# Sliding-window K/V loads as one 128-partition transfer, and four value chunks behind the keys

## The chip, the core and the metric

The kernel runs on one core of one Trainium2 chip; the other cores are idle. The metric is the device time of one launch in microseconds. Five engines matter here: TensorE (PE in the profile), VectorE (DVE), ScalarE (ACT), GpSimd (POOL) and SyncE (SP), which issues nearly all transfers. Sixteen DMA engines carry the transfers between the chip's main memory and the on-chip buffer of 128 partitions.

## The reference

Two attention blocks decode one token for four batches, and their outputs are concatenated. Block A has 32 query heads over 8 key/value heads and looks at the last 2,048 of 8,192 cached positions; block B has 32 key/value heads and looks at all 8,192. The head size is 128.

```
A: W = min(4096, max(256, Sk // 4))                 # 2048
   q = (x @ wq).reshape(B, Sq, Hq, Dh)              # 4, 1, 32, 128
   k = repeat(k_cache[:, :, Sk - W:, :], rep)       # 8 heads, each for 4 query heads
   v = repeat(v_cache[:, :, Sk - W:, :], rep)
   o = softmax(q k^T * Dh ** -0.5) v
   a = o.reshape(B, Sq, Hq * Dh) @ wo               # 4, 1, 512
B: the same with 32 key/value heads, all 8192 positions
return concatenate([a, b], -1)
```

All inputs are bfloat16. The K/V caches that must be read are 33.6 MB for A and 536.9 MB for B; the query and output weights add 8.4 MB each.

## The kernel before

**Chunks.** The work is cut into 72 chunks. Chunks 0 to 7 (A) are one key/value head for all four batches: 64 tiles of 128 positions, 2.10 MB of keys and as much of values. Chunks 8 to 71 (B) are two heads of one batch: 128 tiles, 4.19 MB each of keys and values. A group is eight tiles: 8 groups in an A chunk, 16 in a B chunk.

**Layout.** A partition of a buffer holds 64 consecutive positions of one sequence. In A, batch b lies in partitions 32b to 32b + 31, so a key chunk is loaded by four transfers, one for each batch (L221 to L227). In B two heads take 64 partitions each, and one transfer of 128 partitions loads a chunk (L238).

**For each group** PE transposes eight key tiles into PSUM (`emit_T`, L301), DVE or ACT copies them out (L313 to L317; ACT takes every third), and PE multiplies them with the queries (`emit_S`, L322). A tile's scores are computed against 16 query columns in A (four batches by four heads), and only the columns of a partition's own batch are meant. `scores_out` (L348) therefore copies, for each half chunk, four blocks of 32 partitions with their own four columns.

**Softmax.** `stats_rowmax`, `stats_gmax` and `stats_exp` (L359 to L420) find the maximum over the positions of a row: DVE reduces along the free axis, PE transposes, DVE reduces again, PE spreads the result back. For A, DVE then scales and shifts the scores (L414), ACT takes the exponential in four blocks of 32 partitions (L417), writing each batch's columns into `pba` whose other columns stay zero, and DVE sums over the tiles (L419). The zeros are what keeps the batches apart when PE multiplies values with the probabilities (`emit_pv`, L423), 64 columns at a time of which 16 (A) or 2 (B) are used. `norm_sum`, `norm_out` and `emit_fin` (L443 to L480) divide and multiply with the output weights.

**Order.** The order on PE is written out by group number: transposes of group s, scores of group s - 2, values of an older chunk. Values of a chunk start `PVLAG` groups after the scores end (4 in A, 8 in B). Each engine's queue is in order.

**Buffers.** A ring of ten half-slots of 16 KB a partition (`take`, L184) holds K and V; an A load takes one, a B load two. A load waits until the earlier user of its slot is done: for keys the transposes of their last group, for values the value product. SP issues loads in the order of the list built in L246 to L248: keys of chunk c + 1, then values of chunk c; the values of the last three chunks stand behind all keys. Output weights (`dma_wo`, L209) have three slots: the load for slot use i waits for the product of the chunk that last used it. The first two transfers of query weights use ring slots 8 to 9 and 6 to 7. The last value chunk is loaded in four pieces (64, 32, 16 and 16 tiles, L230 to L237). The values of the third-last chunk may start at group 10 of the last one (L502).

Of the kernel before, what the change touches and what calls it, by code (L numbers as in the profile page):

```python
# [72 lines left out]
def bass_concat_heads__sliding_block_cached__mha_block_cached__decode_kernel(  # L73
        nc, A_x, A_k, A_v, A_wq, A_wo, B_x, B_k, B_v, B_wq, B_wo, out):
    NB = A_x.shape[0]
# [48 lines left out]
    with ExitStack() as es:  # L124
        block = es.enter_context(nc.Block())

        def sb(name, shape, dt):
            return es.enter_context(nc.sbuf_tensor(name, shape, dt))
# [11 lines left out]
        identf = sb("identf", [P, P], F32)  # L140
        onesf = sb("onesf", [P, P], F32)
        onesb = sb("onesb", [P, P], BF16)
        sA = sb("sA", [P, 2, NTA * REP], F32)
        rm = sb("rm", [P, NSM, 4], F32)
        gm = sb("gm", [4, NSM, 4], F32)
        gx = sb("gx", [4, NSM, P], F32)
# [70 lines left out]
        def dma_kv(kind, c):  # L217
            ch = chunks[c]
            T = {("k", 0): A_k, ("k", 1): B_k, ("v", 0): A_v, ("v", 1): B_v}[(kind, ch["ab"])]
            at, waits = take((kind, c), 1 if ch["ab"] == 0 else 2, ("T", ch["s_last"]) if kind == "k" else ("pv", c))  # L220
            if ch["ab"] == 0:  # L221
                PP = P // NB
                for b in range(NB):
                    src = T[b, ch["g"], SkA - W:, :].rearrange("(pp j) d -> pp (j d)", pp=PP)
                    sch.add_dma("sp", lambda e, b=b, src=src: e.dma_start(kv[b * PP:(b + 1) * PP, at, :], src),  # L225
                                "d_h%d" % at, waits=waits, key=(kind, c) if b == NB - 1 else None)
# [18 lines left out]

        loads = [("k", c + 1) for c in range(NC - 1)]  # L246
        for c in range(NC):
            loads.insert(2 * c + 1 if c < NC - 3 else len(loads), ("v", c))  # L248
        wo_next = 0
        for kind, c in loads:  # L250
            dma_kv(kind, c)
# [42 lines left out]
            ms_read[:] = [("q", ab)]  # L294


        def tile_of(kind, c, j):
            at = half_of[(kind, c)]
            return flat(at, chunks[c]["NT"] // NTA)[:, j * P:(j + 1) * P]

        def emit_T(s):  # L301
            c, g = groups[s]
            bank = s % NTRB
            for t in range(TG):
                o = tr[:, bank, t * P:(t + 1) * P]
# [4 lines left out]
                sch.add("pe", lambda e, o=o, i_=i_: e.transpose(o, i_, identb[:, :]),  # L310
                        waits=waits, key=("T", s) if t == TG - 1 else None)
            src, dst = tr[:, bank, :], kt[:, s % NKT, :]
            waits = [("T", s)] + ([("S", s - NKT)] if s >= NKT else [])  # L313
            if s % 3 == 2:
                sch.add("act", lambda e: e.activation(dst, src, ACTF.Copy), waits=waits, key=("ev", s))  # L315
            else:
                sch.add("dve", lambda e: e.tensor_copy(dst, src), waits=waits, key=("ev", s))  # L317

        sc_read = {0: [], 1: []}
        HT = NTA // 2  # L320

        def emit_S(s):  # L322
# [18 lines left out]
                        waits=waits, key=("S", s) if t == TG - 1 else None)  # L341


        def blocks(c):
            U = chunks[c]["U"]
            return [(u, slice(u * (P // U), (u + 1) * (P // U))) for u in range(U)]

        def scores_out(c, half):  # L348

            m = c % 2  # L350
            for u, pp in blocks(c):
                src = sc[pp, half, :].rearrange("p (j x) -> p j x", x=16)[:, :, u * REP:(u + 1) * REP]
                dst = sA[pp, m, half * HT * REP:(half + 1) * HT * REP].rearrange("p (j x) -> p j x", x=REP)
                sch.add("dve", lambda e, src=src, dst=dst: e.tensor_copy(dst, src),  # L354
                        waits=[("S", chunks[c]["s"] + (half + 1) * (HT // TG) - 1)] + ([("exp", c - 2)] if c >= 2 else []),
                        key=("so", c, half) if u == NB - 1 else None)
            sc_read[half] = [("so", c, half)]

        def stats_rowmax(c):  # L359
            ch = chunks[c]  # L360
            m, C = c % NSM, ch["C"]
            if ch["ab"] == 0:
                src = sA[:, c % 2, :].rearrange("p (j c) -> p c j", c=C)
                sch.add("dve", lambda e: e.tensor_reduce(out=rm[:, m, 0:C], in_=src, axis=AX.X, op=ALU.max),
                        waits=[("so", c, 0), ("so", c, 1)], key=("rowmax", c))
                return
            for u, pp in blocks(c):
                src = sc[pp, c % 2, 0:NTB * 2].rearrange("p (j u) -> p u j", u=2)[:, u, :]
                sch.add("dve", lambda e, src=src, pp=pp: e.tensor_reduce(out=rm[pp, m, 0:1], in_=src, axis=AX.X, op=ALU.max),  # L369
                        waits=[("S", ch["s_last"])], key=("rowmax", c) if u == 1 else None)  # L370

        def stats_gmax(c):
            ch = chunks[c]
            m, C, U = c % NSM, ch["C"], ch["U"]
            col = TRM0 + (c % 2) * P
            sch.add("pe", lambda e: e.transpose(ms[0:C, col:col + P], rm[:, m, 0:C], identf[:, :]),  # L376
                    waits=[("rowmax", c), "c_identf"] + ms_read, key=("trm", c))
            src = ms[0:C, col:col + P].rearrange("n (u p) -> n u p", u=U)
# [3 lines left out]
            g = gm[0:C, m, 0:U]  # L382
            gv = bass.AP(g.tensor, g.offset, [g.ap[0], [1, U], [0, P // U]])
            sch.add("dve", lambda e: e.tensor_scalar(out=gx[0:C, m, :].rearrange("n (u p) -> n u p", u=U), in0=gv, scalar1=-scale,  # L384
                                                     scalar2=None, op0=ALU.mult),
                    waits=[("gmax", c)], key=("gx", c))

        def stats_exp(c):
# [10 lines left out]
            pbv = pbt[ab][:, i, 0:ch["NT"] * ch["UC"]].rearrange("p (j x) -> p j x", x=ch["UC"])  # L399
            r = ch["norm"] % NSM  # L400
            if ab == 1:
                for u, pp in blocks(c):
# [9 lines left out]
            nbv = negb[:, m, 0:C]  # L412
            bias = bass.AP(nbv.tensor, nbv.offset, [nbv.ap[0], [0, NTA], [1, C]])
            sch.add("dve", lambda e: e.scalar_tensor_tensor(out=t, in0=t, scalar=scale, in1=bias, op0=ALU.mult, op1=ALU.add),  # L414
                    waits=[("negb", c)], key=("shift", c))
            for u, pp in blocks(c):
                sch.add("act", lambda e, pp=pp, u=u: e.activation(pbv[pp, :, u * C:(u + 1) * C], t[pp], ACTF.Exp),  # L417
                        waits=[("shift", c)] + pw, key=("exp", c) if u == U - 1 else None)
            sch.add("dve", lambda e: e.tensor_reduce(out=rst[0][:, r, :], in_=pbv.rearrange("p j x -> p x j"), axis=AX.X, op=ALU.add),  # L419
                    waits=[("exp", c)] + rs_read[r], key=("rs", c))  # L420


        def emit_pv(c, g):  # L423
# [2 lines left out]
            base = (ch["norm"] % NSM) * 16 + ch["n0"]  # L426
            for t in range(TG):
                j = g * TG + t
                o = po[:, base:base + NW]
                l = tile_of("v", c, j)  # L430
                r = pbt[ch["ab"]][:, c % NPB[ch["ab"]], j * UC:j * UC + NW]
# [60 lines left out]
        for c, ch in enumerate(chunks):  # L492
# [75 lines left out]
```

## Time and profile before

| | |
|---|---|
| median of 3 runs | 1507.73 us (1505.11 to 1511.19) |
| the profiled execution | 1506.58 us |
| its span, first to last instruction | 1504.7 us |
| mean granted TensorE clock | 0.933 |
| PE busy | 1184.0 us (79%) |
| DVE busy | 622.7 us (41%) |
| ACT busy | 443.5 us (29%) |
| POOL busy | 4.5 us (0%) |
| read from main memory | 587.21 MB, 390 GB/s over the span |

The times below come from one execution under the profiler. A page divides the span into 40 slices of 37.6 us; the busy digits are tenths. A row of the table of stages gives, for a stretch from A to B us, the busy time of PE, of its weight loads, of DVE, ACT and POOL with their instruction counts, then the granted clock, the mean busy share of the DMA engines and their rate. A row of the groups gives line, engine, operation, output and input with their shapes, the count, busy time and mean duration, and the idle time of the engine before them with what ended it. A row of the waits gives the waiting engine and line, what released it, the time in total, the number of waits and the longest. A row of the issues gives a transfer, its count, KB each and the median time from issue to landing.

### The profile page before, as it was taken

To read this page: it belongs to the slowest core of one execution; us is meant where nothing else is said; L and a number is where in the kernel's file an instruction comes from. 1 tells how busy PE (TensorE), PEld (TensorE's weight loads), DVE (VectorE), ACT (ScalarE), POOL (GpSimd) and SP (SyncE) were. 2 spreads that over 40 slices of the span, in tenths; PEclk is the share of its full clock that TensorE was granted. 3 is DMA by queue.
4 is the path that set the end of the run, shared out by engine and by line. 5 is a ranking of instruction groups with operands and counts; after the bars stand their busy time and mean duration, and the time that the engine had idled before them with its cause. 6 is when DMAs were issued, how large, how long until landed. Compare 5 with 4: busy or idle time off the path is not lost.

```text
span 1504.7 us, 55575 instructions
## 1 busy us (share of the span) xinstructions
PE 1184.0 (79%) x26704; PEld 1124.8 (75%) x26704; DVE 622.7 (41%) x1211; ACT 443.5 (29%) x651; POOL 4.5 (0%) x12
## 2 busy tenths in 40 slices
PE   3457578878878788887788888788788887888888
PEld 3456468877878788877778877787777877887887
DVE  1344345434444344444444444444444444444443
ACT  0112123322323333332333233233333332332332
POOL 1000000000000000000000000000000000000000
PEclk9677679999999999999999999999999999999999
DMA  9999999999999999999999999999999999999995
GB/s 313 211 215 218 217 339 427 429 429 426 426 428 429 427 424 429 427 427 424 417 421 413 426 426 412 428 412 424 425 418 418 423 425 422 419 419 425 423 424 223
DMA packets 30929, 590.78 MB, mean 393 GB/s; under 512 B 3424, under 2 KB 11632, under 8 KB 11888
## 3 DMA queue, kind: packets, MB, share of 16 engines
q1 hardware_dynamic: 30680, 587.22, 98.2%
q8 instruction: 208, 3.41, 0.9%
q14 instruction: 17, 0.14, 0.0%
q10 hardware_dynamic: 24, 0.01, 0.0%
HBM read 587.21 MB, written 0.01 MB: 390 GB/s over the span
## 4 chain that ended last, share of the span: by engine, by line
DMA 56%; PE 33%; issue 4%; DVE 4%; SPq 2%; another core or an unknown queue 0%; ACT 0%; DVEq 0%
DMA kv<-in_B_k_cache_dram 48%; PE tr L310 15%; PE po L437 8%; PE sc L340 8%; DMA kv<-in_A_k_cache_dram 8%; SPq L225 2%; DVE kt L317 2%; PE ms L392 1%; DVE rm L369 1%; PE ms L376 1%; PE fin L473 0%; DVE rsa L419 0%; ACT pba L417 0%; DVE sA L354 0%
## 5 line engine op out<-in xcount | busy, mean ns | idle before, releaser
L310 PE MATMUL tr<-identb,kv 128*128 128x128 bf16 x8704 | 708.5, 227 | 172.0 <-DMA kv<-in_B_k_cache_dram 83.2
L317 DVE COPY kt<-tr 128x1024 bf16<-128x1024 bf16 x726 | 501.8, 692 | 762.5 <-PE tr L310 759.4
L310 PEld LDWEIGHTS tr<-identb,kv 128*128 128x128 bf16 x8704 | 535.3, 102 | 185.1 <-DMA kv<-in_B_k_cache_dram 89.1
L315 ACT ACTIVATE kt<-tr 128x1024 bf16<-128x1024 bf16 x362 | 370.7, 1024 | 943.8 <-PE tr L310 943.2
L340 PE MATMUL sc<-qs,kt 128*128 128x64 bf16 x8704 | 459.8, 196 | 39.9 <-issue 37.7
L437 PE MATMUL po<-pbb,kv 128*128 128x64 bf16 x8192 | 419.1, 194 | 50.9 <-issue 50.7
L340 PEld LDWEIGHTS sc<-qs,kt 128*128 128x128 bf16 x8704 | 382.8, 101 | 45.2 <-issue 40.1
L437 PEld LDWEIGHTS po<-pbb,kv 128*128 128x128 bf16 x8192 | 319.6, 99 | 63.6 <-issue 63.0
L405 ACT ACTIVATE pbb<-sc,negb 64x128 bf16<-64x128 f32 x128 | 51.5, 402 | 81.8 <-DVE negb L394 80.5
L369 DVE TENSOR_REDUCE rm<-sc 64x1 f32<-64x128 f32 x128 | 36.5, 286 | 17.6 <-PE sc L340 16.7
L376 PE MATMUL ms<-identf,rm 128*1 128x128 f32 (+1 forms) x72 | 20.6, 287 | 20.9 <-DVE rm L369 10.7
L437 PE MATMUL po<-pba,kv 128*128 128x64 bf16 x512 | 32.8, 219 | 1.5 <-issue 1.1
L392 PEld LDWEIGHTS ms<-identf,gx 1*128 1x128 f32 (+1 forms) x144 | 22.2, 192 | 12.4 <-DVE gx L384 6.2
L392 PE MATMUL ms<-identf,gx 1*128 1x1 f32 (+1 forms) x144 | 28.4, 264 | 2.4 <-DVE gx L384 1.8
L437 PEld LDWEIGHTS po<-pba,kv 128*128 128x128 bf16 x512 | 25.7, 115 | 5.2 <-issue 4.7
L473 PE MATMUL fin<-wor,oT 128*4 128x512 bf16 x64 | 18.8, 395 | 13.0 <-DVE oT L453 12.2
L376 PEld LDWEIGHTS ms<-identf,rm 128*1 128x1 f32 (+1 forms) x72 | 6.0, 83 | 30.3 <-DVE rm L369 19.1
L379 DVE TENSOR_REDUCE gm<-ms 1x2 f32<-1x128 f32 (+1 forms) x72 | 19.6, 273 | 13.2 <-PE ms L376 13.2
L405 ACT ACTIVATION_READ_ACCUMULATOR pbb<-sc,negb 64x1 f32 x128 | 23.7, 185 | 0.0
L419 DVE TENSOR_REDUCE rsa<-pba 128x16 f32<-128x1024 bf16 x8 | 15.9, 1993 | 14.0 <-ACT pba L417 14.0
L354 DVE COPY sA<-sc 32x128 f32<-32x128 f32 x64 | 18.2, 285 | 4.9 <-PE sc L340 4.3
L417 ACT ACTIVATE pba<-sA 32x256 bf16<-32x256 f32 x32 | 13.2, 414 | 21.8 <-DVE sA L414 21.3
(31 smaller groups left out, 88.8 us busy)
## 6 DMA issues: line engine op xcount, KB each, us to landing
kv<-in_B_k_cache_dram SPq DMA_DIRECT2D x64, 4096.0 KB, 29.6
kv<-in_B_v_cache_dram SPq DMA_DIRECT2D x63, 4096.0 KB, 32.1
kv<-in_A_k_cache_dram SPq DMA_DIRECT2D x32, 512.0 KB, 38.1
kv<-in_A_v_cache_dram SPq DMA_DIRECT2D x32, 512.0 KB, 41.0
kv<-in_A_wq_dram SPq DMA_DIRECT2D x1, 4096.0 KB, 12.8
kv<-in_B_wq_dram SPq DMA_DIRECT2D x1, 4096.0 KB, 32.9
wor<-in_A_wo_dram SPq DMA_DIRECT2D x8, 512.0 KB, 42.4
wor<-in_B_wo_dram SPq DMA_DIRECT2D x8, 512.0 KB, 32.0
```

What stands on the lines that cost most here:

```text
L225: sch.add_dma("sp", lambda e, b=b, src=src: e.dma_start(kv[b * PP:(b + 1) * PP, at, :], src), "d_h%d" % at, waits=waits, key=(kind, c) if ...
L310: sch.add("pe", lambda e, o=o, i_=i_: e.transpose(o, i_, identb[:, :]), waits=waits, key=("T", s) if t == TG - 1 else None)
L315: sch.add("act", lambda e: e.activation(dst, src, ACTF.Copy), waits=waits, key=("ev", s))
L317: sch.add("dve", lambda e: e.tensor_copy(dst, src), waits=waits, key=("ev", s))
L340: sch.add("pe", lambda e, o=o, l=l, q=q: e.matmul(o, l, q, start=True, stop=True), waits=waits, key=("S", s) if t == TG - 1 else None)
L369: sch.add("dve", lambda e, src=src, pp=pp: e.tensor_reduce(out=rm[pp, m, 0:1], in_=src, axis=AX.X, op=ALU.max), waits=[("S", ch["s_last"]) ...
L376: sch.add("pe", lambda e: e.transpose(ms[0:C, col:col + P], rm[:, m, 0:C], identf[:, :]), waits=[("rowmax", c), "c_identf"] + ms_read, key ...
L379: sch.add("dve", lambda e: e.tensor_reduce(out=gm[0:C, m, 0:U], in_=src, axis=AX.X, op=ALU.max), waits=[("trm", c)], key=("gmax", c))
L392: sch.add("pe", lambda e: e.matmul(ms[:, col:col + C], gx[0:C, m, :], identf[0:C, 0:C], start=True, stop=True), waits=[("gx", c)] + ms_rea ...
L405: sch.add("act", lambda e, src=src, pp=pp, ri=ri, u=u: e.activation(pbv[pp, :, u], src, ACTF.Exp, bias=negb[pp, m, 0:1], scale=scale, accu ...
L437: sch.add("pe", lambda e, o=o, l=l, r=r, j=j: e.matmul(o, l, r, start=(j == 0), stop=(j == ch["NT"] - 1)), waits=waits, key=("pv", c) if j ...
L473: sch.add("pe", lambda e, l=l, r=r, st=st, sp_=sp_: e.matmul(fin[p0:p0 + NB, :], l, r, start=st, stop=sp_), waits=[("oT", c), ("wo", ch["w ...
```

## The change

A sliding chunk is loaded by one transfer of 128 partitions. Partition p now holds batch p mod 4 and the position block p div 4, so the batches are interleaved over the partitions; the rows stay 16 KB. Blocks of 32 partitions can then no longer tell the batches apart, and a mask does it: `mk[p, b]` is 1 where p mod 4 is b. The scores of a half chunk are multiplied with the mask and summed over the four batches (two DVE instructions in place of four copies). ACT takes one exponential of 128 partitions by 256 into a new buffer `eA`; POOL multiplies it with the bfloat16 mask into `pba`, all 16 columns. The sums are taken over `eA` (256 elements a partition) and spread with the mask. The maximum and its spreading follow the new partition order.

Besides, in A every odd group's key copy goes to ACT as well as every third; the lag of A's values goes from 4 to 6 groups; the values of the last four chunks stand behind all keys, start after the last group's transposes, and use 2 columns in place of 64.

```diff
-PVLAG = {0: 4, 1: 8}
+PVLAG = {0: 6, 1: 8}
...
-                PP = P // NB
-                for b in range(NB):
-                    src = T[b, ch["g"], SkA - W:, :].rearrange("(pp j) d -> pp (j d)", pp=PP)
-                    sch.add_dma("sp", lambda e, b=b, src=src: e.dma_start(kv[b * PP:(b + 1) * PP, at, :], src),
-                                "d_h%d" % at, waits=waits, key=(kind, c) if b == NB - 1 else None)
+                src = T[:, ch["g"], SkA - W:, :].rearrange("b (pp j) d -> pp b (j d)", pp=P // NB)
+                sch.add_dma("sp", lambda e: e.dma_start(kv[:, at, :], src), "d_h%d" % at, waits=waits, key=(kind, c))
...
-            loads.insert(2 * c + 1 if c < NC - 3 else len(loads), ("v", c))
+            loads.insert(2 * c + 1 if c < NC - 4 else len(loads), ("v", c))
...
+        idv = identf[:, :].rearrange("p (x b) -> p b x", b=NB)
+        sch.add("dve", lambda e: e.tensor_reduce(out=mk[:, :], in_=idv, axis=AX.X, op=ALU.add), waits=["c_identf"], key="mk")
+        sch.add("dve", lambda e: e.tensor_copy(mkb[:, :], mk[:, :]), waits=["mk"], key="mkb")
...
-            if s % 3 == 2:
+            if s % 3 == 2 or (c < NCA and s % 2 == 1):
...
-            for u, pp in blocks(c):
-                src = sc[pp, half, :].rearrange("p (j x) -> p j x", x=16)[:, :, u * REP:(u + 1) * REP]
-                dst = sA[pp, m, half * HT * REP:(half + 1) * HT * REP].rearrange("p (j x) -> p j x", x=REP)
-                sch.add("dve", lambda e, src=src, dst=dst: e.tensor_copy(dst, src),
...
+            sch.add("dve", lambda e: e.tensor_tensor(
+                out=sel[:, :].rearrange("p (j b c) -> p j b c", b=NB, c=REP),
+                in0=sc[:, half, :].rearrange("p (j b c) -> p j b c", b=NB, c=REP),
+                in1=bcast(mk[:, :], [[0, HT], [1, NB], [0, REP]]), op=ALU.mult),
...
+            sch.add("dve", lambda e: e.tensor_reduce(
+                out=dst, in_=sel[:, :].rearrange("p (j b c) -> p j c b", b=NB, c=REP), axis=AX.X, op=ALU.add),
...
-            for u, pp in blocks(c):
-                sch.add("act", lambda e, pp=pp, u=u: e.activation(pbv[pp, :, u * C:(u + 1) * C], t[pp], ACTF.Exp),
-                        waits=[("shift", c)] + pw, key=("exp", c) if u == U - 1 else None)
-            sch.add("dve", lambda e: e.tensor_reduce(out=rst[0][:, r, :], in_=pbv.rearrange("p j x -> p x j"), axis=AX.X, op=ALU.add),
-                    waits=[("exp", c)] + rs_read[r], key=("rs", c))
+            ev = eA[:, c % 2, :]
+            sch.add("act", lambda e: e.activation(ev, sA[:, c % 2, :], ACTF.Exp),
+                    waits=[("shift", c)] + ([("exp", c - 2), ("rs4", c - 2)] if c >= 2 else []), key=("exp1", c))
+            sch.add("pool", lambda e: e.tensor_tensor(
+                out=pbv.rearrange("p j (b c) -> p j b c", b=NB), in0=bcast(ev, [[C, NTA], [0, NB], [1, C]]),
+                in1=bcast(mkb[:, :], [[0, NTA], [1, NB], [0, C]]), op=ALU.mult),
+                waits=[("exp1", c), "mkb"] + pw, key=("exp", c))
+            sch.add("dve", lambda e: e.tensor_reduce(out=rs4[:, r, :], in_=ev.rearrange("p (j c) -> p c j", c=C), axis=AX.X, op=ALU.add),
+                    waits=[("exp1", c)], key=("rs4", c))
+            sch.add("dve", lambda e: e.tensor_tensor(
+                out=rst[0][:, r, :].rearrange("p (b c) -> p b c", b=NB), in0=bcast(rs4[:, r, :], [[0, NB], [1, C]]),
+                in1=bcast(mk[:, :], [[1, NB], [0, C]]), op=ALU.mult),
+                waits=[("rs4", c)] + rs_read[r], key=("rs", c))
...
-                o = po[:, base:base + NW]
+                n = NW if c < NC - 4 else UC
+                o = po[:, base:base + n]
...
-            if c == NC - 3:
-                v0 = max(v0, chunks[NC - 1]["s"] + 10)
+            if c == NC - 4:
+                v0 = max(v0, chunks[NC - 1]["s_last"] + 1)
```

More of the change, by code (lines that the diff above doesn't have):

```diff
@@ L142, in bass_concat_heads__sliding_block_cached__mha_block_cached__decode_kernel @@
         onesb = sb("onesb", [P, P], BF16)
+        sel = sb("sel", [P, 512], F32)
         sA = sb("sA", [P, 2, NTA * REP], F32)
+        eA = sb("eA", [P, 2, NTA * REP], BF16)
+        rs4 = sb("rs4", [P, NSM, REP], F32)
+        mk = sb("mk", [P, NB], F32)
+        mkb = sb("mkb", [P, NB], BF16)
         rm = sb("rm", [P, NSM, 4], F32)
@@ L319, in bass_concat_heads__sliding_block_cached__mha_block_cached__decode_kernel @@
         sc_read = {0: [], 1: []}
+        sel_read = []
         HT = NTA // 2
@@ L341, in emit_S, with bcast @@
                         waits=waits, key=("S", s) if t == TG - 1 else None)
-        def blocks(c):
-            U = chunks[c]["U"]
-            return [(u, slice(u * (P // U), (u + 1) * (P // U))) for u in range(U)]
+        HALVES = [(0, slice(0, P // 2)), (1, slice(P // 2, P))]
+        def bcast(ap, dims):
+            return bass.AP(ap.tensor, ap.offset, [ap.ap[0]] + dims)
         def scores_out(c, half):
             m = c % 2
-            for u, pp in blocks(c):
-                src = sc[pp, half, :].rearrange("p (j x) -> p j x", x=16)[:, :, u * REP:(u + 1) * REP]
-                dst = sA[pp, m, half * HT * REP:(half + 1) * HT * REP].rearrange("p (j x) -> p j x", x=REP)
[L354 to L357, printed above, removed]
+            sch.add("dve", lambda e: e.tensor_tensor(
+                out=sel[:, :].rearrange("p (j b c) -> p j b c", b=NB, c=REP),
+                in0=sc[:, half, :].rearrange("p (j b c) -> p j b c", b=NB, c=REP),
+                in1=bcast(mk[:, :], [[0, HT], [1, NB], [0, REP]]), op=ALU.mult),
+                waits=[("S", chunks[c]["s"] + (half + 1) * (HT // TG) - 1), "mk"] + sel_read, key=("sel", c, half))
+            sc_read[half] = [("sel", c, half)]
+            dst = sA[:, m, half * HT * REP:(half + 1) * HT * REP].rearrange("p (j c) -> p j c", c=REP)
+            sch.add("dve", lambda e: e.tensor_reduce(
+                out=dst, in_=sel[:, :].rearrange("p (j b c) -> p j c b", b=NB, c=REP), axis=AX.X, op=ALU.add),
+                waits=[("sel", c, half)] + ([("exp1", c - 2)] if c >= 2 else []), key=("so", c, half))
+            sel_read[:] = [("so", c, half)]
         def stats_rowmax(c):
@@ L366, in stats_rowmax @@
                 return
-            for u, pp in blocks(c):
+            for u, pp in HALVES:
                 src = sc[pp, c % 2, 0:NTB * 2].rearrange("p (j u) -> p u j", u=2)[:, u, :]
@@ L377, in stats_gmax @@
                     waits=[("rowmax", c), "c_identf"] + ms_read, key=("trm", c))
-            src = ms[0:C, col:col + P].rearrange("n (u p) -> n u p", u=U)
+            by_row = (lambda x: x.rearrange("n (x u) -> n u x", u=U)) if ch["ab"] == 0 else (lambda x: x.rearrange("n (u x) -> n u x", u=U))
+            src, dst = by_row(ms[0:C, col:col + P]), by_row(gx[0:C, m, :])
             sch.add("dve", lambda e: e.tensor_reduce(out=gm[0:C, m, 0:U], in_=src, axis=AX.X, op=ALU.max),
@@ L381, in stats_gmax @@
             ms_read[:] = [("gmax", c)]
[L382 to L385, printed above, removed]
+            gv = bcast(gm[0:C, m, 0:U], [[1, U], [0, P // U]])
+            sch.add("dve", lambda e: e.tensor_scalar(out=dst, in0=gv, scalar1=-scale, scalar2=None, op0=ALU.mult),
                     waits=[("gmax", c)], key=("gx", c))
@@ L401, in stats_exp @@
             if ab == 1:
-                for u, pp in blocks(c):
+                for u, pp in HALVES:
                     src = sc[pp, c % 2, 0:NTB * 2].rearrange("p (j u) -> p u j", u=2)[:, u, :]
@@ L411, in stats_exp @@
             t = sA[:, c % 2, :].rearrange("p (j c) -> p j c", c=C)
-            nbv = negb[:, m, 0:C]
-            bias = bass.AP(nbv.tensor, nbv.offset, [nbv.ap[0], [0, NTA], [1, C]])
+            bias = bcast(negb[:, m, 0:C], [[0, NTA], [1, C]])
             sch.add("dve", lambda e: e.scalar_tensor_tensor(out=t, in0=t, scalar=scale, in1=bias, op0=ALU.mult, op1=ALU.add),
                     waits=[("negb", c)], key=("shift", c))
-            for u, pp in blocks(c):
-                sch.add("act", lambda e, pp=pp, u=u: e.activation(pbv[pp, :, u * C:(u + 1) * C], t[pp], ACTF.Exp),
-                        waits=[("shift", c)] + pw, key=("exp", c) if u == U - 1 else None)
-            sch.add("dve", lambda e: e.tensor_reduce(out=rst[0][:, r, :], in_=pbv.rearrange("p j x -> p x j"), axis=AX.X, op=ALU.add),
-                    waits=[("exp", c)] + rs_read[r], key=("rs", c))
+            ev = eA[:, c % 2, :]
[11 more added lines that the diff above has]
+                waits=[("rs4", c)] + rs_read[r], key=("rs", c))
         def emit_pv(c, g):
@@ L428, in emit_pv @@
                 j = g * TG + t
[L429 removed]
+                n = NW if c < NC - 4 else UC
+                o = po[:, base:base + n]
                 l = tile_of("v", c, j)
[L431 removed]
+                r = pbt[ch["ab"]][:, c % NPB[ch["ab"]], j * UC:j * UC + n]
                 waits = [("exp", c)] + po_read if j == 0 else []
```

## The prediction

> **What bounds the kernel now.** I read the page's 40 slices first, then the table of stages, to see whether one resource sets the pace throughout.
>
> ```profile
> PEclk9677679999999999999999999999999999999999
> DMA  9999999999999999999999999999999999999995
> GB/s 313 211 215 218 217 339 427 429 429 426 426 428 429 427 424 429 427 427 424 417 421 413 426 426 412 428 412 424 425 418 418 423 425 422 419 419 425 423 424 223
> ...
> 0.00:220.00 220.00, 121.14 (x1926) 110.62 (x1927) 81.24 (x177) 38.08 (x56) 4.47 (x12) 0.74 1.01 248
> 220.00:1480.00 1260.00, 1042.39 (x24225) 995.06 (x24221) 534.11 (x1019) 401.12 (x588) 0.00 (x0) 0.96 1.00 423
> 1480.00:1497.00 17.00, 15.47 (x424) 14.77 (x422) 6.32 (x13) 4.28 (x8) 0.00 (x0) 1.00 0.45 186
> ...
> 40.00:180.00 140.00, 78.15 (x1160) 70.51 (x1160) 57.69 (x127) 26.32 (x40) 0.00 (x0) 0.72 1.02 215
> ```
>
> The last three numbers of a stage row are the granted TensorE clock, the mean busy share of the 16 DMA engines and GB/s. The engines are busy from start to tail, but in two regimes. In the sliding stage (40 to 180 us) they are busy 1.02 of the time and move 215 GB/s; in the full-attention stage, 1.00 of the time and 423 GB/s. All 16 work in both, each at half pace in the first. The compute engines don't cause that: PE works 78.15 of 140 us there, DVE 57.69. The issue list shows how the transfers differ, and the waits of the sliding stage say who is late.
>
> ```profile
> kv<-in_B_k_cache_dram SPq DMA_DIRECT2D x64, 4096.0 KB, 29.6
> kv<-in_A_k_cache_dram SPq DMA_DIRECT2D x32, 512.0 KB, 38.1
> wor<-in_A_wo_dram SPq DMA_DIRECT2D x8, 512.0 KB, 42.4
> ...
> PE tr L310 <- DMA kv<-in_A_k_cache_dram: 43.3, 7, 8.9
> ...
> SPq L215 <- PE sc L340: 8.8, 4, 2.8
> SPq L225 <- PE sc L340: 0.4, 1, 0.4
> ```
>
> A full-attention load writes all 128 partitions (4096 KB); a sliding load is four transfers of 512 KB, each into 32 partitions. PE waits 43.3 us for sliding keys, while SP's semaphore waits there are small (0.4 us at L225, 8.8 us at L215). So the transfers themselves are slow, and their shape is the one difference that the change removes.
>
> **The sliding loads.** Up to 220 us, 220 x 248 = 54.6 MB have moved. At 423 GB/s these take 129.0 us, plus about 2 us before bytes flow: 131 instead of 220, a gain of 89 us. An output-weight load has 1 KB rows and might run slower; one is issued in the full-attention stage at 367.6 and lands about 32 us later:
>
> ```profile
> 367.63 0.44 SPq L215 DMA_DIRECT2D wor<-in_B_wo_dram  x1
> ...
> 390.00:400.00 10.00, 8.30 (x187) 7.60 (x187) 4.32 (x11) 2.96 (x6) 0.00 (x0) 1.00 1.00 419
> ```
>
> 419 against 423 over 10 us is 0.1 us; the eight sliding ones cost 1 us over plain rate. Gain: **88 us**. Ends: zero, if the new transfer is still at half pace; 92, if it reaches the 429 of the best slices.
>
> The new source walks 32 row groups and, inside each, four batches that lie 16 MiB apart (8 heads x 8192 rows x 256 B). No row shows such a pitch; I take 423, as the engines, the partitions and the 128 long rows are those of the full-attention loads. [...]
>
> **Does the faster stream find its buffers?** A sliding chunk moves 2 x 2.10 + 0.52 = 4.72 MB, which is 11.15 us at 423 GB/s. The rows that price PE's side:
>
> ```profile
> 82.18 0.61 PE L310 MATMUL tr<-identb,kv 128*128 128x128 bf16 x8
> 83.09 0.61 PE L310 MATMUL tr<-identb,kv 128*128 128x128 bf16 x8
> ...
> 112.45 1.03 PE L310 MATMUL tr<-identb,kv 128*128 128x128 bf16 x8 [4.81 <-DMA kv<-in_A_k_cache_dram]
> 114.15 1.04 PE L310 MATMUL tr<-identb,kv 128*128 128x128 bf16 x8
> ...
> L317 DVE COPY kt<-tr 128x1024 bf16<-128x1024 bf16 x32 | 22.0, 689 | 59.9 <-PE tr L310 59.8
> L315 ACT ACTIVATE kt<-tr 128x1024 bf16<-128x1024 bf16 x16 | 16.4, 1024 | 96.9 <-PE tr L310 96.8
> L354 DVE COPY sA<-sc 32x128 f32<-32x128 f32 x48 | 13.7, 285 | 3.2 <-PE sc L340 2.7
> L419 DVE TENSOR_REDUCE rsa<-pba 128x16 f32<-128x1024 bf16 x6 | 12.0, 1992 | 10.5 <-ACT pba L417 10.5
> L417 ACT ACTIVATE pba<-sA 32x256 bf16<-32x256 f32 x24 | 9.9, 414 | 16.1 <-DVE sA L414 15.6
> L473 PE MATMUL fin<-wor,oT 128*4 128x512 bf16 x24 | 7.0, 419 | 11.2 <-DVE oT L453 11.2
> L364 DVE TENSOR_REDUCE rm<-sA 128x4 f32<-128x256 f32 x6 | 3.6, 602 | 0.2
> L414 DVE SCALAR_TENSOR_TENSOR sA<-sA,negb 128x256 f32<-128x256 f32 x6 | 2.5, 425 | 0.2
> ```
>
> *PE.* From transpose to transpose a group (transposes, scores, values) takes 0.91 us at full clock (82.18 to 83.09) and 1.70 us at the low clock (112.45 to 114.15). Eight groups: 7.3 us; statistics, sums and output products about 2. So 9.3 us warm.
>
> *Waits.* At the row maximum, DVE today does four copies of 285 ns and a 602 ns reduction after the last scores. The change makes it a masked multiply of 512 (425 ns for 256 two-input elements gives 0.85), a strided reduction of 512 (602 ns for 256 gives 1.2) and the same 0.6: 2.65 us, of which one group's transposes and values (0.7) cover a part: 1.9 us wait. At the output product, 11.2 us over 6 chunks is 1.9 us today, with the 1,992 ns reduction in the way; that one becomes about 0.6 us (256 instead of 1,024 elements), so I put this wait at 0.6. At the first values, the chain is bias copy and shift (0.6), one exponential of 256 (0.41) behind at most one 1.02 us eviction, and POOL's mask multiply. POOL shows only setup:
>
> ```profile
> L176 POOL MEMSET pba<- 128x2176 bf16 x1 | 1.9, 1912 | 0.0
> L167 POOL TENSOR_SCALAR_AFFINE_SELECT identb<-onesb 128x128 bf16<-128x128 bf16 x1 | 0.3, 294 | 0.1
> ```
>
> 0.88 ns an element from the first, 2.3 from the second: 0.9 to 2.35 us for 1,024 elements, and 4.7 if a second input doubles it. I take 2.35, since that row also reads an input. [...] With 0.5 for hand-offs the chain is 4.9 us; the lag of 6 instead of 4 groups leaves four groups (3.65) as cover: 1.2 us. So a chunk costs PE 9.3 + 1.9 + 0.6 + 1.2 = **13.0 us**, from 11.5 to 15.4 with POOL's ends.
>
> *Other engines per chunk.* Two thirds of the evictions go to ACT: 5.3 x 1.02 + 0.41 = 5.9 us. DVE: 2.7 x 0.69 + 2 x 2.05 + 0.6 + about 2 of small work and shift + 0.6 = 9.1 us. Both are under 11.15, so neither sets the rate.
>
> 13.0 is over 11.15, so PE falls behind by about 2 us a chunk, and the question is when SP notices. Ten half-slots hold about five chunk pairs; the tightest wait is the output weights' (slot i waits for the product of chunk i-3), and everything later in SP's queue stands behind it. Both query projections done, PE starts the second chunk near 32 us; the product of chunk c follows (8c+15)/8 chunk times later. By my byte schedule the transfers of output weights 6 and 7 start near 102.6 and 118.7 us and must be issued some 2 us before: 32 + 39p/8 = 100.6 gives p = 14.1, 32 + 47p/8 = 116.7 gives p = 14.4. Below about **14.2 us** a chunk the lag (some 14 us at the end) costs nothing, and PE regains it in the full-attention stage. Above, each us costs 5.9. At 13.0 I charge 1 us for a chunk that starts on the low clock.
>
> **The tail.** The bytes are the same, so after the sliding stage the stream only moves earlier. What follows its end now:
>
> ```profile
> 1496.50:1497.00 0.50, 0.50 (x24) 0.50 (x21) 0.00 (x0) 0.00 (x0) 0.00 (x0) 1.00 0.06 25
> 1497.00:1497.50 0.50, 0.50 (x24) 0.50 (x19) 0.00 (x0) 0.00 (x0) 0.00 (x0) 1.00 0.00 0
> ...
> 1491.41 1.92 PE po L437 x62
> 1493.34 0.31 issue
> 1493.65 6.79 PE po L437 x226
> 1500.64 0.73 PE po L437 x24
> 1501.69 0.61 PE fin L473 x2
> ```
>
> Data end at 1497, but PE is working off values until 1501.4: 226 matmuls in 6.79 us are 30 ns each, three chunks 11.5 us. With four chunks behind the keys, three key chunks come in a row, 9.9 us of transfer each (4.19 MB). PE needs 0.68 us a group without values (0.91 less the value part, 0.24), 10.9 us a key chunk, and 3.8 more where old values are due: it ends the scores about 22 us before the data end, with value chunks then landing at -30, -20, -10 and 0. Nothing waits for a slot: the last value load needs the transposes of the third-last key chunk (-36) and starts at -10. So PE is idle when the last 16 tiles land (0.5 us of matmuls after some 2 us of landing): about 1499.5 instead of 1501.4. Gain **2 us**; from 0, if landing is longer, to 4. Fewer output columns (2 for 64) I cost at nothing, as PE is not the bound there then.
>
> **Sum.** The profiled execution took 1506.58 us (span 1504.7 and 1.9 around it); the median of the three runs is 1507.73, 1.15 more. 1506.58 - 88 + 1 - 2 = 1417.6; I say **1418**.
>
> **The rivals.**
> *PE's chain bounds the sliding stage.* For it: stalls keep the clock low there (0.72), and at 1.70 us a group a chunk costs 13.6 + 2 + 2 = 17.6 us, 3.4 over the threshold: 20 us, time 1438; 1450 at 19.6. Against: the low clock of the rows follows the gaps in which PE waits for keys, and those shrink. Chance 0.14.
> *The four batch rows slow each other.* At half pace the 33.6 MB of sliding K/V take 159 instead of 79 us: 79 us lost, 1497, just short of no change. [...] Chance 0.05.
> *The transfer runs on fewer engines* (it doesn't do what it says). An engine carries 423/16 = 26.4 GB/s. If the inner batch count of four limits the spread, sliding K/V run at 106 GB/s: 317 us for 79, +238, time 1656: **slower**. It decides below 198 GB/s (33.6 MB in 79 + 90 us), i.e. under eight engines. Against: today's 32-row transfers keep the mean of all 16 busy, and the new one starts with the same 32. Chance 0.04.
>
> **Chances and range.** Forecast 0.77 (own range 1408 to 1428), the rivals 0.14, 0.05 and 0.04. A measurement of this kernel tells about 0.5% from no change. Faster by more than that: 0.77 + 0.14 + 0.01 of the pitch rival = 0.92; within 0.5%: 0.03; slower: 0.05. The pitch rival's 0.05 is 0.01 faster, 0.03 the same and 0.01 slower. The range goes from 1408 (1506.58 - 92 - 4 = 1410.6, and 2.6 for the spread of the three runs: 1507.73 less 1505.11) to 1446, most of the first rival.
>
> **What would show it.** Right: the slices of the first 130 us near 420 GB/s; sliding loads of 2048 KB landing in fewer us; key waits of PE in that stage smaller; full-attention slices unchanged; at the end PE idle before the last value pieces. Wrong: 16 engines busy at 215 GB/s again (shape wasn't the cause, or pitch); low DMA share with SP waiting at L215 or for values (PE's chain); a few engines' worth of GB/s. A granted clock at or under 0.72 with long waits at the first values would name POOL's multiply.

## The result and the profile after

| | before | after |
|---|---|---|
| median | 1508.06 us (4 runs, 1505.11 to 1511.19) | 1420.02 us (4 runs, 1419.47 to 1420.90) |
| ratio, 95% interval | | 0.9416 [0.9397, 0.9436] |
| profiled execution | 1506.58 us, span 1504.7 | 1419.47 us, span 1417.6 |

The forecast was 1418 us. The slices of the page after, and the table of stages (last three columns: granted TensorE clock, busy share of the DMA engines, GB/s):

```profile
PEclk8999999999999999999999999999999999999997
DMA  9999999999999999999999999999999999999994
GB/s 400 414 417 422 429 426 429 429 426 430 427 427 426 426 427 432 416 424 429 411 429 426 419 404 431 417 426 415 418 428 427 423 412 416 429 422 408 423 426 206
...
0.00:132.00 132.00, 86.61 (x1902) 77.69 (x1902) 76.07 (x132) 49.22 (x55) 19.63 (x20) 0.96 1.00 413
130.00:1390.00 1260.00, 1044.93 (x24285) 996.05 (x24283) 540.54 (x1029) 403.68 (x592) 1.30 (x1) 0.96 1.00 423
1400.00:1408.00 8.00, 5.38 (x195) 5.30 (x196) 0.00 (x0) 0.00 (x0) 0.00 (x0) 0.50 0.48 198
1408.00:1409.00 1.00, 1.00 (x44) 1.00 (x42) 0.00 (x0) 0.00 (x0) 0.00 (x0) 0.50 0.06 25
1409.00:1417.60 8.60, 5.60 (x155) 4.52 (x152) 1.05 (x3) 0.00 (x0) 0.00 (x0) 0.50 0.01 2
```

The half-speed regime is gone: the first four slices run at 400 to 422 GB/s, where before the first ran at 313 and the next four at 211 to 218. 132 us at 413 GB/s are 54.5 MB, which took 220 us before: 88 us. The full-attention stage is unchanged at 423 GB/s. The last rows are less good: data end between 1408 and 1409 and the span at 1417.6, about 9 us later; before, at 1497 and 1504.7, about 8 us.

PE's rows in the tail of the changed kernel (start, duration, what; in brackets the idle time before and what ended it, "issue" being a wait for nothing that the profile shows):

```profile
1392.04 0.41 PE L349 MATMUL sc<-qs,kt 128*128 128x64 bf16 x8
...
1395.71 3.04 PE L459 MATMUL po<-pbb,kv 128*128 128x2 bf16 x110
1400.26 3.58 PE L459 MATMUL po<-pbb,kv 128*128 128x2 bf16 x128 [1.51 <-issue]
1406.20 3.54 PE L459 MATMUL po<-pbb,kv 128*128 128x2 bf16 x127 [2.36 <-issue]
1409.92 2.78 PE L459 MATMUL po<-pbb,kv 128*128 128x2 bf16 x99 [0.18 <-issue]
1412.99 0.78 PE L459 MATMUL po<-pbb,kv 128*128 128x2 bf16 x24
1414.10 1.01 PE L495 MATMUL fin<-wor,oT 128*4 128x512 bf16 x2 [0.33 <-DVE oT L475]
```

The first row holds the last scores. After it PE is not waiting for values: it runs matmuls in batches of 128 with gaps between, 5.94 us a batch while data flow (1400.26 to 1406.20), and still has 123 to do at 1409.92, when the data are in. A chunk's values are 128 matmuls too, but the batches begin some six matmuls into a chunk, so a landing cannot be what ends the gaps.

### The profile page after: what moved, and what is told of

Same layout as the page of the kernel before. It is cut to its first block, busy times and chain, and to the rows that moved or that the text cites. A ratio compares the mean times of both kernels' runs of the same rounds, so it can differ in the third digit from the quotient of the medians.

```text
span 1417.6 us, 55508 instructions
## 1 busy us (share of the span) xinstructions
PE 1148.0 (81%) x26704; PEld 1088.8 (77%) x26704; DVE 618.3 (44%) x1167; ACT 454.4 (32%) x649; POOL 19.6 (1%) x20
## 3 DMA queue, kind: packets, MB, share of 16 engines
q8 instruction: 208, 3.41, 1.0%
## 4 chain that ended last, share of the span: by engine, by line
DMA 59%; PE 31%; DVE 6%; issue 3%; ACT 0%; SPq 0%; DVEq 0%
DMA kv<-in_B_k_cache_dram 57%; PE tr L318 14%; PE po L459 7%; PE sc L349 7%; DMA kv<-in_A_k_cache_dram 2%; DVE kt L325 2%; DVE sA L368 1%; PE ms L406 1%; DVE rsa L438 1%; PE fin L495 1%; DVE rm L383 1%; PE ms L390 1%; DVE sel L361 1%; DVE rm L378 0%; DVE rs L436 0%
## 5 line engine op out<-in xcount | busy, mean ns | idle before, releaser
L318 PE MATMUL tr<-identb,kv 128*128 128x128 bf16 x8704 | 690.7, 223 | 132.7 <-DMA kv<-in_B_k_cache_dram 96.5
L325 DVE COPY kt<-tr 128x1024 bf16<-128x1024 bf16 x704 | 486.6, 691 | 683.7 <-PE tr L318 680.8
L323 ACT ACTIVATE kt<-tr 128x1024 bf16<-128x1024 bf16 x384 | 392.3, 1024 | 854.8 <-PE tr L318 851.0
L318 PEld LDWEIGHTS tr<-identb,kv 128*128 128x128 bf16 x8704 | 520.0, 100 | 145.1 <-DMA kv<-in_B_k_cache_dram 103.0
L349 PE MATMUL sc<-qs,kt 128*128 128x64 bf16 x8704 | 449.8, 195 | 39.1 <-issue 33.8
L459 PE MATMUL po<-pbb,kv 128*128 128x64 bf16 (+1 forms) x8192 | 413.1, 192 | 43.5 <-issue 41.4
L349 PEld LDWEIGHTS sc<-qs,kt 128*128 128x128 bf16 x8704 | 373.2, 99 | 45.0 <-issue 35.9
L390 PE MATMUL ms<-identf,rm 128*1 128x128 f32 (+1 forms) x72 | 21.0, 291 | 25.3 <-DVE rm L378 14.3
L408 DVE COPY negb<-ms 128x1 f32<-128x1 f32 (+1 forms) x72 | 11.0, 152 | 15.4 <-PE ms L406 15.4
L368 DVE TENSOR_REDUCE sA<-sel 128x128 f32<-128x512 f32 x16 | 16.9, 1059 | 0.5
L399 DVE TENSOR_SCALAR gx<-gm 1x128 f32<-1x128 f32 (+1 forms) x72 | 15.9, 221 | 2.5
```

The source lines that it names most:

```text
L349: sch.add("pe", lambda e, o=o, l=l, q=q: e.matmul(o, l, q, start=True, stop=True), waits=waits, key=("S", s) if t == TG - 1 else None)
L368: sch.add("dve", lambda e: e.tensor_reduce(out=dst, in_=sel[:, :].rearrange("p (j b c) -> p j c b", b=NB, c=REP), axis=AX.X, op=ALU.add), ...
L459: sch.add("pe", lambda e, o=o, l=l, r=r, j=j: e.matmul(o, l, r, start=(j == 0), stop=(j == ch["NT"] - 1)), waits=waits, key=("pv", c) if j ...
```

## The experiments

Times are medians; the kernel before had medians of 1507.0 to 1508.2 beside these runs. The changed kernel is 1420.02.

### What made the sliding loads slow

The old loads had 32 partitions and were small (512 KB). Three runs separate the two. All three keep the interleaved batches of the changed kernel.

```diff
# e5: four transfers of 512 KB again, cut by columns
+                for i in range(4):
+                    x = slice(i * 2048, (i + 1) * 2048)
+                    ... e.dma_start(kv[:, at, x], src[:, :, x])
# e6: cuts = [0, 64, 128]; e7: cuts = [0, 32, 96, 128]
+                for a, z in zip(cuts, cuts[1:]):
+                    ... e.dma_start(kv[a:z, at, :], src[a // NB:z // NB])
```

> The changed kernel, but each sliding chunk again in four transfers of 512 KB, now cut by columns: 128 partitions with 4 KB rows. Theory 1 (the partitions that one transfer reaches set the rate): 1420 to 1425, the stage from 40 to 130 us at 400 GB/s or more. Rival (four small transfers were slow, not their 32 partitions): the old 215 GB/s in that stage and about 1505. A third (the row length counts): something between, below 400 GB/s.

> The changed kernel, each sliding chunk in two transfers of 64 partitions (0 to 63, 64 to 127) with 16 KB rows. [...] Theory 1b (the number of partitions counts, and 64 are enough for 16 engines): 1420 to 1424. Theory 1c (rate in proportion to partitions between 32 and 128): about 300 GB/s, 1455.

> The changed kernel, each sliding chunk in three transfers: partitions 0 to 31, 32 to 95 and 96 to 127. [...] Theory 1c (only the number of partitions counts, with 64 as good or bad as in the run with two halves): the time of that run for the middle part, so 1500 to 1508 if the halves ran at 215 GB/s.

Measured: 1422.78 us by columns, 1502.05 with halves, 1476.67 with 32 to 95 in the middle. The stage row from 40 to 130 us, first of the changed kernel, then of each in this order:

```profile
40.00:130.00 90.00, 66.17 (x1426) 58.19 (x1426) 64.02 (x114) 40.67 (x46) 13.85 (x8) 1.00 1.02 417
```

```profile
40.00:130.00 90.00, 67.44 (x1379) 58.74 (x1380) 62.92 (x111) 39.70 (x44) 13.24 (x7) 0.96 1.04 406
```

```profile
40.00:130.00 90.00, 48.09 (x742) 42.95 (x742) 34.97 (x60) 23.83 (x26) 7.57 (x4) 0.71 1.02 227
```

```profile
40.00:130.00 90.00, 56.38 (x958) 50.12 (x959) 44.00 (x77) 29.17 (x32) 9.46 (x5) 0.80 0.77 273
```

Four small transfers of 128 partitions run at 406 GB/s against 417 in the changed kernel, so neither size nor count was the cause. Two transfers of 64 partitions run at 227, close to the old 215, although each has twice the partitions. Sixty-four partitions from 32 to 95 raise the rate to 273: it is not how many partitions a transfer has, but which. (That a transfer into one end of the buffer is followed by one into the other is not the reason; so it is in the run with halves, at 227.) What partitions 32 to 95 have over 0 to 63 no run shows. By the number of partitions alone (theory 1c) the third run should have taken as long as the one with halves, 1502.05 us; it took 1476.67. Its engines are busy only 0.77 of the time, where those of the other two runs are busy throughout (1.04 and 1.02); why was not tried.

### How much of PE's lag is hidden

`p` is the time of a sliding chunk on PE, read as the mean distance from one transpose of the row maximum to the next, first to seventh. In the changed kernel:

```profile
39.09 0.27 PE L390 MATMUL ms<-identf,rm 128*4 128x128 f32 x1 [1.64 <-DVE rm L378]
...
113.85 0.27 PE L390 MATMUL ms<-identf,rm 128*4 128x128 f32 x1 [1.81 <-DVE rm L378]
...
109.46 0.37 SPq L221 DMA_DIRECT2D wor<-in_A_wo_dram  x1
```

(113.85 - 39.09) / 6 = 12.5 us; the expectations below took 13.2, which is the distance of single pairs only. The last row is SP's issue of the last sliding output weights; 116.7 us is the time by which the prediction wanted it. Two runs lengthen the chain before that transpose, one undoes the change's two small edits.

```diff
# e9: one, e8: four extra masked multiplies of the second half chunk
+            for i in range(n if half == 1 else 0):
+                sch.add("dve", lambda e: e.tensor_tensor(out=sel..., in0=sc..., in1=mk..., op=ALU.mult), ...
# e10
-PVLAG = {0: 6, 1: 8}
+PVLAG = {0: 4, 1: 8}
-            if s % 3 == 2 or (c < NCA and s % 2 == 1):
+            if s % 3 == 2:
```

> The changed kernel with the masked multiply of the second half chunk done five times instead of once (same result): 4 x 0.67 = 2.7 us more in the row maximum's chain of each sliding chunk, so p goes from 13.2 (measured from one maximum to the next) to 15.9. Theory 1 (the prediction's threshold of 14.2 us and 5.9 us for each us above): 1420 + 10 = 1430. Rival (no slack, each us is paid in each of eight chunks): 1441. Rival (PE's lag in the sliding stage is hidden altogether): 1420.

> As the run with four extra masked multiplies, but one: 0.67 us more for a sliding chunk, p about 13.9 instead of 13.2. Theory 1 (a threshold, 14.2 us by the prediction, below which SP's queue hides PE's lag): 1420, within 1 us of the changed kernel. Rival (no slack; the four extra ones cost 21.9 us for 4.0 us of p, so 5.5 for each us from 13.2 on): 1423.5 to 1425.5.

> The changed kernel with the two small edits undone: sliding values start 4 instead of 6 groups behind the scores, and ACT takes every third key copy there instead of four in six. The first values then wait for the mask multiply (two groups, 1.8 us, less cover) and DVE gets 2.7 copies of 0.69 us more a chunk. If both add up, p goes from 13.2 to about 15 and the rule says 5 us: 1425. If they hide behind each other, p stays under 14.2: 1420. Rival (both edits carry much of the gain): over 1435.

| run | p, us | last sliding output weights issued, us | median, us | over 1420.02 |
|---|---|---|---|---|
| changed kernel | 12.5 | 109.5 | 1420.02 (1419.47 to 1420.90) | |
| e10, lag 4 and thirds | 13.9 | 115.2 | 1419.92 (1418.18 to 1425.93) | -0.1 |
| e9, one extra | 14.3 | 120.3 | 1421.93 (1419.66 to 1424.70) | 1.9 |
| e8, four extra | 16.7 | 135.1 | 1441.95 (1441.44 to 1442.80) | 21.9 |

The rows of the first and the seventh maximum in e10, e9 and e8, from which p comes, and the issue; for e8 also a later issue and three stage rows:

```profile
39.42 0.37 PE L390 MATMUL ms<-identf,rm 128*4 128x128 f32 x1 [1.89 <-DVE rm L378]
...
122.56 0.27 PE L390 MATMUL ms<-identf,rm 128*4 128x128 f32 x1 [2.79 <-DVE rinv L469]
...
115.20 0.37 SPq L221 DMA_DIRECT2D wor<-in_A_wo_dram  x1
```

```profile
39.85 0.27 PE L396 MATMUL ms<-identf,rm 128*4 128x128 f32 x1 [2.37 <-DVE rm L384]
...
125.38 0.27 PE L396 MATMUL ms<-identf,rm 128*4 128x128 f32 x1 [2.53 <-DVE rm L384]
...
120.28 0.37 SPq L221 DMA_DIRECT2D wor<-in_A_wo_dram  x1
```

```profile
42.16 0.37 PE L396 MATMUL ms<-identf,rm 128*4 128x128 f32 x1 [4.67 <-DVE rm L384]
...
142.35 0.37 PE L396 MATMUL ms<-identf,rm 128*4 128x128 f32 x1 [4.72 <-DVE rm L384]
...
135.06 0.37 SPq L221 DMA_DIRECT2D wor<-in_A_wo_dram  x1
...
167.57 0.33 SPq L241 DMA_DIRECT2D kv<-in_B_k_cache_dram  x1
...
80.00:120.00 40.00, 28.81 (x505) 25.28 (x503) 26.88 (x47) 13.85 (x16) 3.79 (x2) 0.83 0.67 264
120.00:170.00 50.00, 34.11 (x571) 30.06 (x568) 33.76 (x58) 14.84 (x17) 5.68 (x3) 0.76 0.84 335
...
160.00:170.00 10.00, 10.00 (x146) 9.04 (x144) 4.75 (x9) 2.46 (x3) 1.89 (x1) 0.65 0.45 159
```

There is a threshold: 1.4 us more a chunk (e10) cost nothing, so the two small edits carry none of the gain; 4.2 us more cost 22, and then the DMA engines do run short (busy 0.67, 264 GB/s) as the prediction described. The issue times agree: the issue is 1.5 us before 116.7 in e10 and 18.4 us after it in e8.

The rule's size was missed: e8 was put at 1430, and with the measured p the rule gives 1435, not 1442. The rival "no slack" named 1441 for e8 and is right there only by chance. It had counted 2.7 us for each of eight chunks, while p rose by 4.2: with gaps of 4.7 us the granted clock is 0.83 and 0.76 in e8's stage rows, where the changed kernel has 1.00, and a maximum's transpose takes 0.37 instead of 0.27 us. With the measured p this rival asks for 34 us in e8, and for 11 in e10. e9 alone is unclear; its runs span both expectations.

### The tail

```diff
# e1: the old tail on the new loads
-            loads.insert(2 * c + 1 if c < NC - 4 else len(loads), ("v", c))
+            loads.insert(2 * c + 1 if c < NC - 3 else len(loads), ("v", c))
-                n = NW if c < NC - 4 else UC
+                n = NW
-            if c == NC - 4:
-                v0 = max(v0, chunks[NC - 1]["s_last"] + 1)
+            if c == NC - 3:
+                v0 = max(v0, chunks[NC - 1]["s"] + 10)
# e2: only n = NW; e3: NC - 5 for NC - 4 in all three places
# e4
+                if c >= NC - 4 and t % 2 and ("vl", j) not in sch.tk and j != ch["NT"] - 1:
+                    continue
```

> The new sliding loads stay; the tail is as before (three value chunks behind the keys, started at group 10 of the last key chunk, 64 columns). Theory 1 (PE is the bound at the end, because its instructions arrive no faster than about 128 matmuls in 5.9 us while data flow; the order of the last loads then matters little): the end lies about 7.7 us behind the end of the data as in the kernel before, so 1417 to 1419 us, 1 to 2 below the changed kernel's 1420.0. Theory 2 (the prediction: with four value chunks last PE waits for data, and the order gives 2 us): 1422.

> The changed kernel with 64 instead of 2 columns in the last four chunks' value matmuls. Theory 1 (number of matmuls counts, not their width): 30 instead of 28 ns each, but the clock stays up, so 1419 to 1420.5 and the granted clock of the tail near 1.0 instead of 0.5. Rival (the low clock in the tail, which the narrow matmuls bring, costs the end): 1417.5 to 1418.5. If narrow matmuls were worth something: 1423 or more.

> The changed kernel with five instead of four value chunks behind all keys. Theory 1: PE still has all its matmuls to do and gets one more chunk of values late, in the stretch where a block of 128 takes 5.9 us: 1420 to 1424. Rival (four keys in a row let PE finish the scores earlier against the end of the data, so that it then waits for values): 1416 to 1418.

> The changed kernel in which about every second value matmul of the last four chunks is left out (about 254 of 512; the result of these four chunks is not the reference's, the loads are all there). Theory 1: about two blocks of 128 fewer in the tail, so the end is set by the last piece of data (1408 in the trace, 2 us of landing, 0.3 of matmuls, 3.8 behind): 1415 to 1416.5. Theory 2 (landing of values sets the end): 1419.5 to 1420.5, no change.

Measured: 1418.36 us with the old tail (1417.64 to 1419.35), 1420.48 with wide matmuls, 1420.27 with five chunks last, 1415.32 with half of the value matmuls (1415.19 to 1416.33). All four lie in theory 1's ranges. With half of the matmuls waits for data appear in PE's rows of the tail; the longest of them, and the end:

```profile
1404.36 0.99 PE L461 MATMUL po<-pbb,kv 128*128 128x2 bf16 x32 [2.17 <-DMA kv<-in_B_v_cache_dram]
1409.95 1.01 PE L497 MATMUL fin<-wor,oT 128*4 128x512 bf16 x2 [0.33 <-DVE oT L477]
```

So in the changed kernel the number of matmuls left at the end sets the end, not the landing of values. The new tail is worth nothing or costs 1.7 us: the runs of the old tail and of the changed kernel (1419.47 to 1420.90) don't overlap, but the difference is close to their spread. Wide matmuls keep the clock at 1.00 from 1400 to 1408 us, where the changed kernel has 0.50, and still don't shorten the tail.

### A version that is faster than both

If key chunks in a row put PE behind, the keys can lead earlier and all the way, so that four value chunks stand last without a row of keys.

```diff
-            loads.insert(2 * c + 1 if c < NC - 4 else len(loads), ("v", c))
+            loads.insert(2 * c + (1 if c < NCA else 3), ("v", c))    # e12; e11: 2
-PVLAG = {0: 6, 1: 8}
+PVLAG = {0: 6, 1: 42}                                                # e12; e11: 26
-                n = NW if c < NC - 4 else UC
+                n = NW
-            if c == NC - 4:
-                v0 = max(v0, chunks[NC - 1]["s_last"] + 1)
```

> Another order of all full-attention loads: keys of chunk c + 2, then values of chunk c, all the way, so that three value chunks stand behind the last keys without two or three key chunks in a row; values start 26 groups behind the scores, 64 columns. Theory 1 (PE comes to the last chunk late because key chunks in a row give it more matmuls than it gets instructions for): the end within 5 to 7 us of the end of the data instead of 9.4: 1416 to 1417.5. Rival (PE's matmuls are behind whatever the order): 1418 to 1420, as with three values last after keys in a row.

> The same with keys three chunks ahead, so that four value chunks stand behind the last keys; values start 42 groups behind the scores. Theory 1: 1415.5 to 1417 (the run with half of the last value matmuls left out, 1415.3, is near the floor that the data set). Rival: 1418 to 1420; and if keys so far ahead run short of slots, over 1422.

Measured: 1418.66 us with a lead of two (1418.29 to 1418.82), 1416.31 with three (1415.39 to 1417.90; ratio to before 0.9397 [0.9380, 0.9415]). The lead of two gave only what the old tail gives: theory 1's range was missed. The lead of three falls into it, 3.7 us (0.26%) under the changed kernel, and the two sets of runs don't overlap; against the old tail (e1) it is 2.0 us, and there they do. Its tail:

```profile
1395.96 3.92 PE L459 MATMUL po<-pbb,kv 128*128 128x64 bf16 x128 [1.33 <-issue]
1401.90 5.43 PE L459 MATMUL po<-pbb,kv 128*128 128x64 bf16 x127 [2.02 <-issue]
1407.83 3.06 PE L459 MATMUL po<-pbb,kv 128*128 128x64 bf16 x99 [0.50 <-issue]
1410.95 0.86 PE L459 MATMUL po<-pbb,kv 128*128 128x64 bf16 x24
1412.14 0.59 PE L495 MATMUL fin<-wor,oT 128*4 128x512 bf16 x2 [0.33 <-DVE oT L475]
```

The first two batches still begin 5.9 us apart, but the last begins at 1407.83 instead of 1409.92: PE entered the tail 2 us earlier. Whether the order alone did this, or the later start of values as well, was not separated, and why a lead of two is not enough stays open.

## Why the prediction was right, and where it was not

**The sliding loads (88 us): right in mechanism and size.** 88 us by the stage rows. The three runs on the shape (406, 227 and 273 GB/s) show that the partitions a transfer reaches were the cause, which the prediction had only as the one difference left. Its first rival, PE's chain as the bound, did not come either: from 40 to 130 us the granted clock is 1.00 and p is 12.5 us.

**The pitch rival did not come.** Rows 16 MiB apart run at 400 to 422 GB/s; the slower first slices are within 6% of the later ones' 423. The rival of fewer engines is out by the same rows.

**PE's side (13.0 us a chunk): 12.5 measured, with wrong terms that offset each other.** Groups and waits of the changed kernel's sliding stage:

```profile
L361 DVE TENSOR_TENSOR sel<-sc,mk 128x512 f32<-128x512 f32 x16 | 10.6, 665 | 11.6 <-PE sc L349 11.6
L368 DVE TENSOR_REDUCE sA<-sel 128x128 f32<-128x512 f32 x16 | 16.9, 1059 | 0.5
L432 POOL TENSOR_TENSOR pba<-eA,mkb 128x1024 bf16<-128x1024 bf16 x8 | 15.2, 1894 | 110.9 <-ACT eA L430 99.9 <-PE sc L349 11.0
...
PE ms L390 <- DVE rm L378: 14.3, 8, 1.8
...
PE fin L495 <- DVE oT L475: 6.4, 6, 1.5
PE sc L349 <- DVE kt L325: 4.6, 5, 1.6
```

The masked multiply took 0.67 us (0.85 assumed) and the reduction 1.06 (1.2); the wait at the maximum 14.3/8 = 1.8 (1.9). POOL's multiply took 1.89 us (2.35 assumed), and no row shows PE waiting for it (1.2 charged). Against these, the wait at the output product was 6.4/6 = 1.1 us (0.6), and PE waited 4.6 us (0.6 a chunk) for DVE's key copies, which had no term. So the half microsecond between 13.0 and 12.5 owes something to luck. The low end of the prediction's range, 11.5, should be 11.8 by its own terms (13.0 less the 1.2). The microsecond charged for a first chunk on the low clock has no row of its own.

**The threshold (14.2 us and 5.9 us for each above): right in kind, the slope too small.** SP's wait stood where it was put, at the output weights:

```profile
SPq L221 <- PE fin L495: 56.3, 6, 11.6
```

It costs nothing at 12.5: the last of these issues comes at 109.46 us, 7 us before the 116.7 of the prediction. From the e9 and e8 points the slope is 20.0/2.4 = 8.3 us for each microsecond, and the line reaches zero at 14.3 - 1.9/8.3 = 14.0; as e9 spreads over 5 us, both are rough. The prediction priced the wait of the last sliding output weights alone (47/8 chunks). That issue did move as it said, by 14.8 us from e9 to e8, or 6.1 for each microsecond of p. The time moved by 20.0, as later slots were late as well: in e8 SP issues a full-attention key load only at 167.57, and the DMA engines are busy 0.45 of the 10 us from 160 to 170. How much each wait cost was not separated.

**The tail (2 us gained): wrong.** Nothing was gained, and perhaps 1.7 us lost. The failing step is "PE is idle when the last 16 tiles land". Its term was 30 ns a matmul, 3.8 us a value chunk, from 226 matmuls of the kernel before that begin 3 us before its data end. While data flow, 128 matmuls take 5.9 us, and the rows of before have the same beat ahead of those 226:

```profile
1487.71 0.56 PE L310 MATMUL tr<-identb,kv 128*128 128x128 bf16 x7 [0.25 <-issue]
...
1493.65 6.79 PE L437 MATMUL po<-pbb,kv 128*128 128x64 bf16 x226 [0.31 <-issue]
```

So PE ended its scores at 1392, 16 us before the data end instead of 22, and had some 500 of the last 512 value matmuls left. Narrower columns were worth nothing, as costed (1420.48 in e2 with wide ones), but not for the reason given: PE is the bound there.

**The total** came out 2 us off, as the tail's error, 2 to 4 us, is small beside 88 and is partly met by the microsecond charged to the sliding stage, which no row shows. That part of the closeness is luck.

## What to carry to other kernels

When all DMA engines are busy and the rate is half of what it is elsewhere, look at which partitions a transfer covers before its size: here 64 partitions from 0 or from 64 ran at 227 GB/s and 32 at 215, while 512 KB pieces over all 128 were nearly as fast as 2 MB (406 and 417). A lag of an engine behind the stream was free only up to the slots in hand (1.4 us more a chunk cost nothing, 4.2 us cost 22); find the first wait in the issuing queue, compare its time with the time at which the transfer is due, and expect later waits to add to it. At the end of a stream that sets the pace, count what the compute engines still have to issue while the last transfers land, at the rate that they reach while data flow (here 128 matmuls in 5.94 us).

## What was not expected of the hardware

**Batches of 128 matmuls.** PE's gaps put down to "issue" end every 128 matmuls in the changed kernel's tail (at 1400.26, 1406.20 and 1409.92). The queue of the page that carries instructions moved

```profile
q8 instruction: 208, 3.41, 1.0%
```

3.41 MB in 208 packets. PE ran 26,704 matmuls and as many weight loads: 53,408 instructions, 257 for each packet, or 128 matmuls with their weight loads; the some 2,100 instructions of the other engines are left aside. The two counts agree so well that the gaps look like waits for the next packet of instructions behind the bulk loads: batches begin 5.9 us apart while data flow, and once the data are in, the gap shrinks to 0.18 us (at 1409.92). This is an estimate from these counts; no run changed the instruction stream's transfers. e4 shows that fewer matmuls shorten the end.

**A DVE instruction that ends with POOL's.** The smallest new DVE instruction, 16 elements at L438, took 1.51 us:

```profile
52.36 0.42 DVE L436 TENSOR_REDUCE rs<-eA 128x4 f32<-128x256 bf16 x1 [0.48 <-ACT eA L430]
52.41 1.90 POOL L432 TENSOR_TENSOR pba<-eA,mkb 128x1024 bf16<-128x1024 bf16 x1 [8.76 <-ACT eA L430]
52.82 1.51 DVE L438 TENSOR_TENSOR rsa<-rs,mk 128x16 f32<-128x16 f32 x1
```

It ends at 54.33, with POOL's multiply (54.31), while the reduction before it, beside the same POOL instruction, took 0.42 us (0.6 assumed). All eight such instructions (1.51 to 1.52 us) end 0.02 to 0.04 us after POOL's multiply of their chunk. That they wait for POOL is my reading of these ends; no run moved either. The prediction gave this instruction next to nothing; it holds DVE for 12 us in all (eight times 1.51), and p stays below the threshold, so it costs nothing here.

**Half of the engines' time at the end.** In the last 16 us before the data end the DMA engines are busy 0.44 of the time before (1481 to 1497 us) and 0.48 after (1392 to 1408). Whether some of them finish early, or all run at half pace, and why, stays open. The prediction's landing times for the last value chunks (-30, -20, -10 and 0) took the full rate to the end.
